# A fused transformer layer on one core: the softmax sums inverted three units later, the maxima split on VectorE, the next heads' operands loaded in parts

## The chip, the core and the metric

The kernel runs on one core of a Trainium2 chip. The core has five engines that each run their own instruction list in order and wait for one another by semaphores: TensorE (PE, matrix products; PEld is its weight load), VectorE (DVE), ScalarE (ACT), GpSimd (POOL) and SyncE (SP). SyncE computes nothing here: it issues all the DMA transfers, one after the other. TensorE writes to PSUM, which has eight banks of 128x512 float32; everything else lies in SBUF or in DRAM. The metric is the device time of one execution in microseconds (us).

## The reference

The layer adds three things to its input x (2048 rows, 512 columns): attention with 32 heads of width 16, a two-layer network with GELU (hidden width 1792), and x itself. Both branches read the same normalised x.

```
xn = layernorm(x)
qkv = (xn @ wqkv) in 32 heads of 16
p = softmax(q k^T * 16**-0.5) over 2048 keys;  o = p @ v
attention = o @ wo
mlp = gelu(xn @ w1 + b1) @ w2 + b2
out = x + attention + mlp
```

## The kernel before

**Precision.** Matrix operands are float16 pairs, a high part and the low part that it leaves, so that three products make one. Weights are scaled by powers of two from their largest value before they are split.

**Blocks and units.** Attention goes through eight groups of four heads, and within a group through four query blocks of 512 rows: 32 blocks, numbered t = 0 to 31. A block has 16 *units*. A unit (`unit`, L584) does two things. Its S half (`s_half`, L238) makes four 128x512 score tiles by TensorE and takes each one's row maxima by VectorE (L250): this is the first pass, which only finds the maxima. Its E half (`e_half`, L286) belongs to a block 20 units behind (`LEAD`): TensorE makes the scores again, transposed and with the maximum already subtracted, ScalarE takes the exponential (L297), and TensorE multiplies the result with v (`v_half`, L300), where a column of ones makes the sums of the exponentials as well. Between these halves TensorE gets a few products of the dense work (projections first, then the network's hidden and output layer, then the output projection).

**How the maxima get into the E half.** The operands of a group lie in SBUF "stacks" kst and qst (L79), 62 rows of q or k parts for the products, and two rows per head (62 and 63) that hold the maximum's two float16 parts in qst and a constant, 1024, in kst. At a block's last S unit `s_end` (L253) reduces the maxima to mneg (L261). One unit later `store` (L264) transposes mneg by TensorE into PSUM, VectorE scales it into msb (L271), GpSimd makes the high part and the low part, mhl (L274, L275), SyncE writes them to DRAM, m_d (L277, two transfers), and reads them back into rows 62 and 63 of qst (L282, four transfers). The block's E half needs these rows some four units later; its score products wait for qst<-m_d.

**How a block's sums are inverted.** When a block's last product with v is done, `v_end` (L313) copies the result to osb by ScalarE (L323) and sets up a chain with a due time for each step, counted in units: the sums to DRAM (L335) after 1, reshaped back into dn (L362) after 2, the inversion on VectorE (L338) after 2 + n, its result to DRAM (L340) one later, spread to rb (L344) after 3 + 2n, and then `store` (L346) after 4 + 3n: GpSimd multiplies osb by rb (L348), makes the float16 pair ot (L349, L350), and n units later `put` writes ot to DRAM, ot_d (L355, four transfers). n is 2, and 1 for the last four blocks.

**What sets the order.** TensorE, ScalarE, VectorE and GpSimd execute in the order in which the program issues their instructions. `later(n, f)` (L204) puts a step n units off, `tick` (L226) runs what is due, and `pooled` (L216) feeds GpSimd's steps by a budget of 2500 ns a unit. SyncE is not in this list (`ORDERED`, L40): the order of its transfers is made by the scheduler when the program is built, from its own idea of when operands and buffers become free; at run time the queue is strictly in order.

**Loading the stacks.** `stacks(g, w, blocks)` (L389) loads one operand of one group, four transfers of 48 KB a block. The stacks are held twice, for even and odd groups. Group 0 is loaded in the prologue; group 1, all 32 transfers, by the first call of `rest` (L855), which then writes the normalised x to DRAM, xn_d, in four transfers of 512 KB (L859); groups 2 to 7 by `more_stacks` (L1043), 32 transfers at once, when the E half has left the group that used the buffers.

**The prologue.** Units 0 to 15 (S only) run between the first projections. While they run, the weights pass by once in chunks (wch, L646) for their largest values (L650 on VectorE), and later once more to be split on GpSimd (L877 to L879). Units 16 to 19 have no E half yet; TensorE gets bursts of 8 to 16 products there.

Of the kernel before, what the change touches and what calls it, by code (L numbers as in the profile page):

```python
# [8 lines left out]
F32 = mybir.dt.float32  # L9
# [3 lines left out]
ALU = mybir.AluOpType  # L13
# [14 lines left out]
NQB = S // QB  # L28
NG = H // 4
VW = DH + 1  # L30
LEAD = 20
# [11 lines left out]
MROW = 1024.0  # L43
# [4 lines left out]
def layer_kernel(ctx: ExitStack, tc: tile.TileContext, x, wqkv, wo, w1, b1, w2, b2, out):  # L48
    nc = tc.nc
# [3 lines left out]
    def pool(stack, name, bufs=1, space=None, side=None):  # L53
        kw = {k: v for k, v in (("space", space), ("side", side)) if v is not None}
        return stack.enter_context(tc.tile_pool(name=name, bufs=bufs, **kw))

    const = pool(ctx, "const")
    work = pool(ctx, "work")
# [5 lines left out]
    xn_d = dram.tile([P, 2, NC, S], F16, name="xn_d")  # L64
# [42 lines left out]
    def banks(tag):  # L107
        k = free_banks[tag].pop(0)
        free_banks[tag].append(k)
        return bank_tile(k, tag)  # L110
# [48 lines left out]
    def given(engine, ns):  # L159
        backlog[engine] += ns  # L160
# [43 lines left out]
    def later(n, fn, local=False):  # L204
        queue.append((slot[0] + n, fn, local))
# [10 lines left out]
    def pooled(*todo):  # L216
        steps.extend(todo)
# [35 lines left out]
    def s_end(u):  # L253

        t, i = divmod(u, 16)
        if i < 15:
            return
        g, qb = divmod(t, NQB)
        qs = qst[g % 2]
        mneg = mnegs[t % 2]  # L260
        nc.vector.tensor_reduce(mneg[:, :16], mt_of[t].rearrange("p h t k -> p (h t) k"), axis=AX.X, op=ALU.max, negate=True)  # L261
        given("dve", 220)

        def store():  # L264

            pt = banks("S")
            for a in range(2):
                nc.tensor.matmul(pt[32 * a:32 * a + 32, :64], mneg[64 * a:64 * a + 64, :],
                                 ident[64 * a:64 * a + 64, 64 * a:64 * a + 64], start=True, stop=True)
            msb = work.tile([64, 64], F32, name="msb", bufs=2)  # L270
            nc.vector.tensor_scalar_mul(msb, pt[:64, :64], 1.0 / MROW)  # L271
            given("dve", 220)
            mhl = work.tile([64, 2, 64], F16, name="mhl", bufs=2)
            nc.gpsimd.tensor_scalar(mhl[:, 0], msb, 1.0, 0.0, op0=ALU.mult, op1=ALU.add)  # L274
            nc.gpsimd.tensor_tensor(mhl[:, 1], msb, mhl[:, 0], op=ALU.subtract)  # L275
            for a in range(2):
                nc.sync.dma_start(m_d[t, :, :, 64 * a:64 * a + 64], mhl[32 * a:32 * a + 16])  # L277
            for p in range(2):
                for a in range(2):
                    h = 2 * p + a  # L280
                    dst = qs[p][qb][64 * a + 62:64 * a + 64, :].rearrange("r (t q) -> r t q", q=P)
                    nc.sync.dma_start(dst, m_d[t, 4 * h:4 * h + 4].rearrange("t r q -> r t q"))  # L282

        later(1, store)
# [28 lines left out]
    def v_end(u):  # L313

        t, kt = divmod(u, 16)
        g, qb = divmod(t, NQB)
        for h in range(4):
            del ptiles[u, h]
        if kt < 15:
            return  # L320
        pv, k = pv_of.pop(t)
        osb = work.tile([P, QB], F32, name="osb", bufs=2)
        nc.scalar.activation(osb, pv, AF.Copy)  # L323
        given("act", 600)
        free_banks["S"].append(k)
        if t == NG * NQB - 1:
            later(1, lambda: last_one(osb))
            return

        dn = work.tile([64, 32], F32, name="dn", bufs=1)  # L330
        rb = work.tile([P, QB], F32, name="rb", bufs=1)

        def sums():
            for h in range(4):
                nc.sync.dma_start(den_d[t, 0, h:h + 1, :], osb[32 * h + DH:32 * h + DH + 1, :])  # L335

        def inverse():
            nc.vector.reciprocal(dn, dn)  # L338
            given("dve", 330)
            later(1, lambda: nc.sync.dma_start(den_d[t, 1].rearrange("h (c q) -> (h c) q", q=32), dn))  # L340

        def spread():
            for h in range(4):
                nc.sync.dma_start(rb[32 * h:32 * h + 32, :], den_d[t, 1, h:h + 1, :].to_broadcast([32, QB]))  # L344

        def store():  # L346
            ot = work.tile([P, 2, QB], F16, name="ot", bufs=2)
            pooled((1280, lambda: nc.gpsimd.tensor_tensor(osb, osb, rb, op=ALU.mult)),  # L348
                   (620, lambda: nc.gpsimd.tensor_scalar(ot[:, 0], osb, 1.0, 0.0, op0=ALU.mult, op1=ALU.add)),  # L349
                   (1160, lambda: nc.gpsimd.tensor_tensor(ot[:, 1], osb, ot[:, 0], op=ALU.subtract)),  # L350
                   (0, lambda: later(n, put)))

            def put():
                for h in range(4):
                    nc.sync.dma_start(ot_d[64 * g + DH * h:64 * g + DH * h + DH, :, qb * QB:(qb + 1) * QB],  # L355
                                      ot[32 * h:32 * h + DH])
                ready.add(t)


        n = 2 if t < (NG - 1) * NQB else 1  # L360
        later(1, sums)
        later(2, lambda: nc.sync.dma_start(dn, den_d[t, 0].rearrange("h (c q) -> (h c) q", q=32)))  # L362
        later(2 + n, inverse)
        later(3 + 2 * n, spread)
        later(4 + 3 * n, store)

    def last_one(osb):

        on = work.tile([P, 4, 4, DH], F32, name="on")
        rden = work.tile([P, 4, 4], F32, name="rden")  # L370
        pq = banks("S")
        for q in range(4):
            nc.tensor.transpose(pq[:, q * P:(q + 1) * P], osb[:, q * P:(q + 1) * P], ident)
        pqv = pq.rearrange("p (q h e) -> p q h e", q=4, h=4)
        nc.vector.reciprocal(rden, pqv[:, :, :, DH])
        nc.vector.tensor_tensor(on, pqv[:, :, :, 0:DH], rden.unsqueeze(3).to_broadcast([P, 4, 4, DH]), op=ALU.mult)
        pt = banks("S")
        for q in range(4):
            nc.tensor.transpose(pt[:64, q * P:(q + 1) * P], on[:, q].rearrange("p h d -> p (h d)"), ident)
        ot = work.tile([P, 2, QB], F16, name="ot", bufs=2)  # L380
        nc.scalar.activation(ot[:64, 0], pt[:64, :], AF.Copy)
        nc.vector.tensor_tensor(ot[:64, 1], pt[:64, :], ot[:64, 0], op=ALU.subtract)
        last.append(ot)
# [5 lines left out]
    def stacks(g, w, blocks):  # L389
        for b in blocks:  # L390
            for p in range(2):
                for a in range(2):
                    h = 4 * g + 2 * p + a
                    nc.sync.dma_start((qst, kst)[w][g % 2][p][b][64 * a:64 * a + 48, :],
                                      qk_d[w, h * DH:(h + 1) * DH, :, b * QB:(b + 1) * QB].rearrange("d j n -> (d j) n"))
# [69 lines left out]
    def by_slots(gen):  # L465

        def step():
            w = FINE
            while w == FINE:
                w = next(gen, 0)  # L470
            if w is None:
                later(1, step, True)

        later(1, step, True)
# [56 lines left out]
    pos, spent, cur = [0], [False], [None]  # L531
# [7 lines left out]
    def fetch_w1(n):  # L539
        if n < NQB * NF:  # L540
            wcs[n] = feed[0].tile([P, 2, NC, P], F16, name="wc", bufs=3)
            nc.sync.dma_start(wcs[n], w1_d[n % NF])
# [89 lines left out]
    with ExitStack() as st1:  # L632
# [3 lines left out]
        xt = ph.tile([P, 2, NC, S], F16, name="xt")  # L636
# [216 lines left out]
        feed.append(pool(ctx, "feed", side="right"))  # L853

        def rest():  # L855
            for w in (1, 0):
                stacks(1, w, range(NQB))
            for c in range(NC):
                nc.sync.dma_start(xn_d[:, :, c, :], xt[:, :, c, :])  # L859
            for m in range(1, 4):  # L860
                while m not in ready_w:
                    yield None
                if m < 3:
                    by_slots(prep_qk(m + 1, wfs[m + 1], sbank, ready_w))
                for sb in range(NQB):
                    for w in (1, 0):
                        yield project(m, w, sb, ready_w[m], dbank)
                    if m == 3 and sb == 2:
                        for n in range(2):
                            fetch_w1(n)  # L870
                        fetch_x(0)
# [166 lines left out]
                        lambda q=q: (yos[q], None), lambda yo, q=q: finish(yo, acs[q], qb * 4 + q), first=False)  # L1038

    yos = []  # L1040
    loaded = [1]

    def more_stacks():  # L1043

        e = pos[0] - LEAD
        while loaded[0] + 1 < NG and e > (loaded[0]) * 64:
            loaded[0] += 1
            for w in (1, 0):
                stacks(loaded[0], w, range(NQB))

    with ExitStack() as st2:
        st2p = pool(st2, "ph2")
# [5 lines left out]
    with ExitStack() as st3:  # L1058
# [35 lines left out]
        while pos[0] < NU + LEAD + 2:  # L1094
            more_stacks()
            unit(fil)
# [32 lines left out]
```

## Time and profile before

| | us |
|---|---|
| median of three runs | 1570.55 |
| lowest, highest run | 1565.78, 1573.75 |
| the profiled execution's own time | 1564.4 |
| its span, first to last instruction | 1562.6 |
| VectorE busy, of it row maxima (L250, 2048 instructions) | 1419.0, 1289.1 |
| ScalarE busy, of it exponentials (L297, 2048 instructions) | 1369.2, 1267.6 |
| GpSimd busy | 668.9 |

The mean granted clock of TensorE was 0.992 of full speed. Rows of the profile name an instruction by line, engine, operation and "out<-in" with the program's names; in lists of waits, "A <- B: 11.9, 3, 5.5" says that A waited for B 11.9 us in all, 3 times, 5.5 at most. In the timeline a row gives start, duration, engine, line, operation, shapes and count, and in brackets the idle time of the engine before it with what ended it. SyncE's rows are DMA issues; SPq is its sequencer. In rows by stretch, the columns are the stretch, its length, the busy time of PE, PEld, DVE, ACT and POOL (with counts), the granted clock, the share of the DMA engines and GB/s.

### The profile page before, as it was taken

What the parts mean: (1) busy time and instruction counts of PE and PEld (TensorE: products, weight loads), DVE (VectorE), ACT (ScalarE), POOL (GpSimd) and SP (SyncE); (2) the same over time, 40 slices, a digit from 0 to 9 for tenths busy, and PEclk for the clock granted to TensorE, in tenths of its full rate; (3) what the DMA queues carried; (4) which work ended last, traced back from release to release, by engine and by line L of the source; (5) the groups of instructions that cost most, each with busy time, mean ns of one, the idle gap of its engine ahead of it and who ended that gap; (6) DMA issues with size and microseconds to landing.
All of it is one profiled execution on the core that took longest, in us unless ns stands there. A gap on an engine that the chain in (4) does not pass through costs nothing.

```text
span 1562.6 us, 85974 instructions
## 1 busy us (share of the span) xinstructions
PE 1509.6 (97%) x38915; PEld 813.5 (52%) x38915; DVE 1419.0 (91%) x2388; ACT 1369.2 (88%) x2254; POOL 668.9 (43%) x742
## 2 busy tenths in 40 slices
PE   8997998989999999999999999999999999999998
PEld 4433554545555555555555555555555555554543
DVE  8886987989999999999999999999999999999911
ACT  4314997989999999999999999999999999999993
POOL 3113587737773111777411167751127773111000
PEclk9998999999999999999999999999999999999999
DMA  6467466351121111121111111221112100003123
GB/s 205 129 205 257 130 172 211 114 167 47 47 67 50 38 34 36 58 57 44 55 44 50 34 45 43 64 63 37 40 41 66 42 21 28 29 21 125 55 91 103
DMA packets 120248, 123.71 MB, mean 79 GB/s; under 512 B 38988, under 2 KB 90572, under 8 KB 119880
## 3 DMA queue, kind: packets, MB, share of 16 engines
q1 hardware_dynamic: 119880, 118.21, 25.0%
q8 instruction: 304, 4.98, 1.3%
q14 instruction: 64, 0.52, 0.1%
HBM read 80.61 MB, written 37.34 MB: 75 GB/s over the span
## 4 chain that ended last, share of the span: by engine, by line
PE 70%; DVE 21%; DMA 4%; issue 2%; POOL 1%; SPq 1%; ACT 1%; DVEq 0%; POOLq 0%
PE pV L169 21%; DVE mt L250 16%; PE pD L169 16%; PE pS L169 15%; PE pT L169 14%; DVE hh L978 2%; PE pD L428 1%; DMA wch<-in_B_w_dram 1%; PE pT L428 1%; DVE amx L650 1%; DMA dn<-den_d 1%; PE pT L521 1%; DMA m_d<-mhl 0%; PE pS L428 0%; DMA out_dram<-ac 0%
## 5 line engine op out<-in xcount | busy, mean ns | idle before, releaser
L297 ACT ACTIVATE pe<-pT,sexp 128x512 f32<-128x512 f32 x2048 | 1267.6, 688 | 72.8 <-PE pT L169 26.9
L250 DVE TENSOR_REDUCE mt<-pS 128x1 f32<-128x512 f32 x2048 | 1289.1, 683 | 34.4 <-PE pS L169 15.6
L169 PE MATMUL pV<-pe,vv 64*32 64x512 f32 x8192 | 1079.0, 597 | 1.4 <-PE pS L169 0.7
L169 PE MATMUL pT<-qst,kst 64*32 64x512 f16 x8192 | 706.9, 379 | 3.9 <-DMA qst<-m_d 1.4
L169 PE MATMUL pS<-kst,qst 62*32 62x512 f16 x8192 | 636.1, 379 | 35.6 <-DVE mt L250 32.1
L169 PEld LDWEIGHTS <-qst 62*32 62x32 f16 x8192 | 280.2, 92 | 273.5 <-issue 136.2
L169 PEld LDWEIGHTS <-kst 64*32 64x32 f16 x8192 | 294.1, 91 | 176.5 <-issue 68.6
L169 PE MATMUL pD<-w_s,g 64*32 64x512 f16 x5376 | 364.8, 377 | 0.0
L169 PE MATMUL pD<-xb,wc 64*32 64x512 f16 x5376 | 361.4, 378 | 0.0
L169 PEld LDWEIGHTS pV<-pe,vv 64*32 64x32 f32 x8192 | 181.6, 105 | 96.7 <-PE pS L169 7.6
L169 PEld LDWEIGHTS <-wc 64*32 64x32 f16 x5376 | 120.5, 92 | 52.6 <-issue 2.7
L169 PEld LDWEIGHTS <-g 64*32 64x32 f16 x5376 | 111.4, 91 | 44.4 <-issue 0.2
L169 PE MATMUL pD<-xt,wqk_h 64*32 64x512 f16 x1920 | 127.4, 382 | 0.7 <-issue 0.7
L996 POOL TENSOR_TENSOR xa<-xa,yt 128x512 f32<-128x512 f32 x16 | 20.4, 1276 | 238.8 <-ACT yt L994 238.8
L958 POOL TENSOR_TENSOR t<-hh 128x512 f32<-128x512 f32 x56 | 58.2, 1038 | 112.0 <-DVE hh L978 110.7
L348 POOL TENSOR_TENSOR osb<-osb,rb 128x512 f32<-128x512 f32 x31 | 39.9, 1286 | 150.5 <-DMA rb<-den_d 150.5
L274 POOL TENSOR_SCALAR mhl<-msb 64x64 f16<-64x64 f32 x32 | 7.6, 237 | 175.4 <-DVE msb L271 175.4
L960 POOL TENSOR_TENSOR t<-t,hh 128x512 f32<-128x512 f32 x56 | 71.7, 1280 | 4.7
L953 POOL TENSOR_TENSOR t<-t,hh 128x512 f32<-128x512 f32 x56 | 71.6, 1279 | 4.7
L955 POOL TENSOR_TENSOR g<-t,g 128x512 f16<-128x512 f32 x56 | 65.1, 1163 | 4.6
L169 PEld LDWEIGHTS <-wqk_h 64*32 64x32 f16 x1920 | 43.8, 93 | 16.1 <-issue 1.3
L169 PE MATMUL pD<-wo_s,oc 64*32 64x512 f16 x768 | 50.1, 378 | 0.0
(138 smaller groups left out, 869.5 us busy)
## 6 DMA issues: line engine op xcount, KB each, us to landing
wch<-in_B_w_dram SPq DMA_DIRECT2D x28, 512.0 KB
wc<-w_d SPq DMA_DIRECT2D x56, 256.0 KB
qk_d<-stg SPq DMA_DIRECT2D x32, 256.0 KB
rb<-den_d SPq DMA_DIRECT2D x124, 64.0 KB
kst<-qk_d SPq DMA_DIRECT2D x128, 48.0 KB
qst<-qk_d SPq DMA_DIRECT2D x128, 48.0 KB
xs<-in_A_x_dram SPq DMA_DIRECT2D x16, 256.0 KB
qk_d<-stg SPq DMA_DIRECT2D x32, 128.0 KB
```

Source lines behind the costliest of these rows:

```text
L169: p = nc.tensor.matmul(*args, **kw)
L250: nc.vector.reduce_max(mt_of[t][:, n, qt, kb:kb + 1], s, axis=AX.X)
L297: nc.scalar.activation(pe, st, AF.Exp, scale=sexp[:, g // 2:g // 2 + 1])
L348: pooled((1280, lambda: nc.gpsimd.tensor_tensor(osb, osb, rb, op=ALU.mult)), (620, lambda: nc.gpsimd.tensor_scalar(ot[:, 0], osb, 1.0, 0.0 ...
L428: nc.tensor.matmul(self.bank, lhs, rhs, start=start, stop=self.last and self.over())
L521: nc.tensor.matmul(pj, xt[:, i, c, t * P:(t + 1) * P], wh[j][:, c, :], start=(n == 0), stop=(n == 11))
L953: (1280, lambda: nc.gpsimd.tensor_tensor(t1, t1, hh, op=ALU.mult)),
L955: (1160, lambda: nc.gpsimd.tensor_tensor(g[:, 1, f, :], t1, g[:, 0, f, :], op=ALU.subtract)),
L958: pooled((1040, lambda: nc.gpsimd.tensor_tensor(t1, hh, hh, op=ALU.mult)), (620, lambda: nc.gpsimd.tensor_scalar(t1, t1, 1.0, 1.0 / GELU_A ...
L960: (1280, lambda: nc.gpsimd.tensor_tensor(t1, t1, hh, op=ALU.mult)),
L978: nc.vector.tensor_scalar(hh, hp, scale, bias, op0=ALU.mult, op1=ALU.add)
L996: add = lambda: nc.gpsimd.tensor_tensor(xa, xa, yt, op=ALU.add)
```

## The change

Three edits:

1. In `v_end` the inversion, its spreading and the product with it come three units later, in all but the last four blocks. The steps keep their distances from the inversion on; the sums' way to dn is not moved.
2. In `store` of the maxima, VectorE makes both float16 parts straight from PSUM: the high part by the scaling that made msb, the low part by a second instruction that scales the same PSUM values again and subtracts the high part. msb and GpSimd's two steps are gone. The book-keeping of VectorE's load (`given`) goes from 220 to 300 ns.
3. The stacks of a next group are loaded in eight parts, four transfers a unit, k's four blocks first. For group 1 that is from the first unit after the prologue on, with the four xn_d writes behind it, one a unit; for the later groups from three units after the E half has entered a group.

```diff
@@ s_end, store
-            msb = work.tile([64, 64], F32, name="msb", bufs=2)
-            nc.vector.tensor_scalar_mul(msb, pt[:64, :64], 1.0 / MROW)
-            given("dve", 220)
             mhl = work.tile([64, 2, 64], F16, name="mhl", bufs=2)
-            nc.gpsimd.tensor_scalar(mhl[:, 0], msb, 1.0, 0.0, op0=ALU.mult, op1=ALU.add)
-            nc.gpsimd.tensor_tensor(mhl[:, 1], msb, mhl[:, 0], op=ALU.subtract)
+            nc.vector.tensor_scalar_mul(mhl[:, 0], pt[:64, :64], 1.0 / MROW)
+            nc.vector.scalar_tensor_tensor(mhl[:, 1], pt[:64, :64], 1.0 / MROW, mhl[:, 0], op0=ALU.mult, op1=ALU.subtract)
+            given("dve", 300)
@@ v_end
-        n = 2 if t < (NG - 1) * NQB else 1
+        n, far = (2, 3) if t < (NG - 1) * NQB else (1, 0)
         later(1, sums)
         later(2, lambda: nc.sync.dma_start(dn, den_d[t, 0].rearrange("h (c q) -> (h c) q", q=32)))
-        later(2 + n, inverse)
-        later(3 + 2 * n, spread)
-        later(4 + 3 * n, store)
+        later(2 + n + far, inverse)
+        later(3 + 2 * n + far, spread)
+        later(4 + 3 * n + far, store)
@@ rest
-            for w in (1, 0):
-                stacks(1, w, range(NQB))
+            for k in range(8):
+                later(1 + k, lambda k=k: stacks(1, 1 - k // 4, [k % 4]), True)
             for c in range(NC):
-                nc.sync.dma_start(xn_d[:, :, c, :], xt[:, :, c, :])
+                later(9 + c, lambda c=c: nc.sync.dma_start(xn_d[:, :, c, :], xt[:, :, c, :]), True)
@@ more_stacks
-    loaded = [1]
+    loaded = [0]
...
-        e = pos[0] - LEAD
-        while loaded[0] + 1 < NG and e > (loaded[0]) * 64:
+        g, k = divmod(loaded[0], 8)
+        if g + 2 < NG and pos[0] - LEAD >= 64 * (g + 1) + 3:
             loaded[0] += 1
-            for w in (1, 0):
-                stacks(loaded[0], w, range(NQB))
+            stacks(g + 2, 1 - k // 4, [k % 4])
```

In the changed program as built, the lines after these edits stand up to three lines higher.

## The prediction

> **What bounds the kernel now.** I read the page first, then the waits by engine, then the timeline around the longest waits of VectorE, and last the queue of SyncE. "Unit" is the step of the schedule in which four 128x512 score tiles are reduced (S) and four tiles of a block 20 units behind are exponentiated (E); a "block" is sixteen units (front section).
>
> ```profile
> PE 1509.6 (97%) x38915; PEld 813.5 (52%) x38915; DVE 1419.0 (91%) x2388; ACT 1369.2 (88%) x2254; POOL 668.9 (43%) x742
> 390.00:440.00 50.00, 49.08 (x1399) 27.04 (x1400) 49.56 (x84) 47.97 (x81) 38.21 (x42) 1.00 0.16 43
> 520.00:570.00 50.00, 49.91 (x1402) 28.49 (x1396) 49.25 (x82) 48.26 (x80) 6.08 (x7) 1.00 0.11 32
> ```
>
> The two stretches (us; then PE, PEld, DVE, ACT, POOL busy) show a kernel without slack: in the hidden-layer stage (390 to 440) VectorE works 49.56 of 50 us, in the output-layer stage (520 to 570) TensorE 49.91. Every engine runs a fixed order, so a wait of TensorE or VectorE in a unit is lost for good, nearly in full. What can be won are the few idle times:
>
> ```profile
> DVE dn L338 <- DMA dn<-den_d: 11.9, 3, 5.5
> DVE amx L650 <- DMA wch<-in_B_w_dram: 9.3, 2, 8.3
> ```
>
> (engine and line, what it waited for, us in all, times, longest.) Two of the three waits for dn and one for a weight chunk are long; the rest of the span is dense. SyncE's queue has waits of its own, and these will matter:
>
> ```profile
> SPq L355 <- POOL ot L350: 154.7, 27, 14.3
> ```
>
> SyncE stands 154.7 us at L355, in 27 blocks, until GpSimd has finished ot. It issues in order: whatever is behind waits as well. Today that harms little.
>
> **The change, part by part.** The sum is made against the profiled execution, 1564.4 us (span 1562.6); the median of the three runs, 1570.55, lies 6.15 above it.
>
> *Loads of the next heads in parts.* SyncE's order is chosen by the scheduler as operands become free, and in the built programs the stack loads of the later head groups hardly change places. What does change is the start: the four xn_d writes, today ahead of a weight chunk and of the first m_d, go behind the first qst<-m_d; the chunk goes ahead of all sixteen qst loads.
>
> ```profile
> 106.20 7.39 SPq L394 DMA_DIRECT2D qst<-qk_d  x16
> 113.64 4.14 SPq L859 DMA_DIRECT2D xn_d<-xt  x4
> 117.87 1.33 SPq L646 DMA_DIRECT2D wch<-in_B_w_dram  x1
> ...
> 129.22 0.69 DVE L650 TENSOR_REDUCE amx<-wch 128x1 f32<-128x512 f32 x1 [8.29 <-DMA wch<-in_B_w_dram]
> ...
> 118.93 2.77 PE L428 MATMUL pT<-xt,wqk_h 128*128 128x512 f16 x12
> ...
> 131.11 4.56 PE L428 MATMUL pD<-xt,wqk_h 128*128 128x512 f16 x12
> ```
>
> The chunk is issued at 117.87 and lands at 129.22; VectorE idles 8.29 us. Issued near 106, it has over 14 us before VectorE wants it at 120.9, against the 11.35 us that it took even behind all the other transfers: the wait goes. After it twelve products took 4.56 us, the same twelve before it 2.77: 1.79 more. Gain 8.29 + 1.79 = **10.1**. What is late next is the first E unit's qst<-m_d, wanted 10.1 us sooner than today; the xn_d writes no longer stand in front of it. Bounds: 6 (I allow it to be late by 4) to 11.4 (the whole landing time is won).
>
> *Inversion three units later.* Sums, inversion, spread and product of a block all keep their distances; inversion, spread, product and the ot_d writes move by three units.
>
> ```profile
> 249.77 0.53 SPq L362 DMA_DIRECT2D dn<-den_d  x1
> ...
> 255.13 0.34 DVE L338 RECIPROCAL dn<-dn 64x32 f32<-64x32 f32 x1 [5.52 <-DMA dn<-den_d]
> ...
> 258.89 1.29 DVE L250 TENSOR_REDUCE mt<-pS 128x1 f32<-128x512 f32 x2 [1.08 <-PE pS L169]
> 261.35 2.02 DVE L250 TENSOR_REDUCE mt<-pS 128x1 f32<-128x512 f32 x3 [1.17 <-PE pS L169]
> ...
> 348.87 0.35 DVE L338 RECIPROCAL dn<-dn 64x32 f32<-64x32 f32 x1 [4.94 <-DMA dn<-den_d]
> ...
> 352.63 0.69 DVE L250 TENSOR_REDUCE mt<-pS 128x1 f32<-128x512 f32 x1 [1.08 <-PE pS L169]
> ```
>
> Three units are 8 us (the m_d rows of blocks 18 and 19 below lie 44.69 us apart, sixteen units of 2.79), more than 5.52 or 4.94: both waits go, and with them the slow matmuls behind them. Gain 5.52 + 1.08 + 1.17 + 4.94 + 1.08 = **13.8**; not below 11 (half of the after-effects stays). The third wait, about 1.4, is in one of the last four blocks, which keep their distances.
>
> *Maxima's parts on VectorE.* Per block one VectorE instruction more, reading PSUM and the part before it, and two fewer on GpSimd.
>
> ```profile
> L271 DVE TENSOR_SCALAR msb<-pS 64x64 f32<-64x64 f32 x32 | 6.8, 212 | 5.5 <-PE pS L268 2.5 <-PE pT L169 1.7 <-PE pS L169 0.7
> L338 DVE RECIPROCAL dn<-dn 64x32 f32<-64x32 f32 x31 | 10.4, 335 | 11.9 <-DMA dn<-den_d 11.9
> ```
>
> No row has this form. The nearest, L271, is 212 ns; it is at hand in 32 blocks, and VectorE is the limit in about ten (the hidden-layer stage): 10 x 0.21 = **2.1** lost. Ends: 32 x 0.335 = 10.7 with L338's price everywhere; below nothing by 3, if the shorter way to m_d (GpSimd ends mhl 0.70 us behind msb) helps blocks whose E waits today.
>
> *What the later inversion pushes.* This is where I differ from reading the change as a gain. In the changed order the four ot_d writes of block t-2 stand ahead of the m_d writes of block t in most blocks, as today, but their data now comes 8 us later, and m_d is what the E stage of block t needs. Block 19 today:
>
> ```profile
> 966.32 1.17 POOL L350 TENSOR_TENSOR ot<-osb,ot 128x512 f16<-128x512 f32 x1
> 970.59 0.24 POOL L274 TENSOR_SCALAR mhl<-msb 64x64 f16<-64x64 f32 x1 [3.10 <-DVE msb L271]
> ...
> 967.51 2.48 SPq L355 DMA_DIRECT2D ot_d<-ot  x4
> ...
> 971.23 1.50 SPq L277 DMA_DIRECT2D m_d<-mhl  x2
> 974.33 1.18 SPq L282 DMA_DIRECT2D qst<-m_d  x4
> ...
> 978.95 1.26 ACT L297 ACTIVATE pe<-pT,sexp 128x512 f32<-128x512 f32 x2
> ```
>
> ot is ready at 967.5, its writes are out at 970.0, and m_d leaves at 971.23 as soon as mhl is there. Put the product at 972.2 and ot at 975.4 (three units on; in the changed GpSimd order one more run of GELU steps stands ahead of the product): the writes take 2.48, m_d leaves at 977.9, 6.7 late. The room: qst<-m_d ends its issue at 975.51, E begins at 978.95, 3.44 later. How much of that the landing needs is shown by block 18, where today two ot_d writes stand between m_d and qst<-m_d:
>
> ```profile
> 926.54 1.23 SPq L277 DMA_DIRECT2D m_d<-mhl  x2
> 930.86 1.18 SPq L355 DMA_DIRECT2D ot_d<-ot  x2
> 932.14 1.30 SPq L282 DMA_DIRECT2D qst<-m_d  x4
> ...
> 933.88 0.10 PEld L169 LDWEIGHTS <-kst 64*32 64x32 f16 x4 [1.52 <-DMA qst<-m_d]
> ...
> 934.54 0.69 DVE L250 TENSOR_REDUCE mt<-pS 128x1 f32<-128x512 f32 x1 [0.73 <-PE pS L169]
> 935.62 1.29 DVE L250 TENSOR_REDUCE mt<-pS 128x1 f32<-128x512 f32 x2 [0.39 <-PE pT L169]
> ```
>
> There the product begins 0.44 after the issue's end, its exponential some 0.5 later: the landing needs 1.0, the room in block 19 is 2.4, and TensorE waits 6.7 - 2.4 = 4.3. Block 18 also shows the price: TensorE's loader waits 1.52, VectorE loses 0.73 + 0.39 = 1.12, so 0.4 of each wait is absorbed. I carried this subtraction through all blocks, with each block's own rows and the changed orders of GpSimd and SyncE. First and last of thirteen:
>
> ```profile
> 370.33 1.19 SPq L277 DMA_DIRECT2D m_d<-mhl  x2
> 374.78 1.18 SPq L282 DMA_DIRECT2D qst<-m_d  x4
> ...
> 378.06 1.27 ACT L297 ACTIVATE pe<-pT,sexp 128x512 f32<-128x512 f32 x2
> ...
> 1276.03 1.18 SPq L277 DMA_DIRECT2D m_d<-mhl  x2
> 1279.90 1.15 SPq L282 DMA_DIRECT2D qst<-m_d  x4
> ...
> 1283.05 1.94 ACT L297 ACTIVATE pe<-pT,sexp 128x512 f32<-128x512 f32 x3
> ```
>
> Block 5: ot at 374.5, m_d 6.7 late, room 1.1, wait 5.6. Block 26: ot at 1277.0, 3.5 late, room 1.0, wait 2.5. All: blocks 5, 7, 8, 11, 12, 14, 16, 18, 19, 21, 24, 25, 26 wait 5.6, 4.7, 3.5, 1.5, 5.0, 1.3, 0.3, 0.4, 4.3, 1.8, 5.0, 2.4, 2.5 = 38.3 (in 11, 18 and 25 it is qst<-m_d that stands behind an ot_d write). In the others ot comes in time, or the writes stand behind qst<-m_d. Less 13 x 0.4 = 5.2.
>
> Waits also cool the clock. After the idle times of 5.2 and 4.7 us that the dn waits gave TensorE, the granted clock (third column from the end) was low:
>
> ```profile
> 256.00:261.00 5.00, 4.92 (x80) 2.33 (x83) 3.10 (x6) 2.44 (x4) 1.52 (x2) 0.50 0.60 168
> 349.50:354.00 4.50, 4.18 (x80) 1.96 (x79) 3.34 (x6) 1.94 (x3) 0.00 (x0) 0.62 0.25 71
> ```
>
> It cost 2.25 and 1.08 there. Five of the thirteen waits are 4.3 or more; I count a quarter of them at 1.7: 2. The Trainium skill ("TensorE: Matmul & The Clock Gate", Part 1) has the clock halved after an idle window of about 3.4 us that runs free of the program. By that rule alone all five could be hit, and the term would be 8.5 in place of 2; the two rows agree with the rule, but no row here shows what an idle time of about 4 us does.
>
> Term: 38.3 - 5.2 + 2 = **35.1** lost, from 12 (only blocks whose m_d is 6 or more late) to 50 (the bare shift of three units, without GpSimd's new order, in every block).
>
> Sum: 1564.4 - 10.1 - 13.8 + 2.1 + 35.1 = 1577.7, 13.3 more than before; on the median 1570.55 + 13.3 = **1584**.
>
> **The rivals.**
>
> *The writes are out in time.* GpSimd loses its wait for msb (3.10 in the row above), and the product could start as soon as rb has landed. It decides from the point where the product starts as many us sooner as TensorE would wait: in block 19 4.3 sooner than 972.2, and m_d is late by no more than the room. For it speaks that the product waits for rb alone where no GELU steps stand ahead; against it, that in the changed GpSimd order they do. Then only 10.1 + 13.8 - 2.1 = 21.8 of gain is left: 1549, faster.
>
> *Half absorbed.* If the landing needs less than 1.0, or GpSimd catches up after the first waits, the term is 15 in place of 35.1, the sum 13.3 - 20.1 = -6.8: 1564 on the median, no change.
>
> *The start isn't won.* If the chunk is held by the transfers and not by its place, or the first qst<-m_d is late, 10.1 is missing: 1594.
>
> *The inversion still waits.* If dn comes over 8 us late, the change doesn't do what it says: 13.8 is missing, 1598. Against it: 5.52 is the longest of 31.
>
> **How the numbers follow.** Forecast 0.55; writes in time 0.13; half absorbed 0.15; start not won 0.12; inversion waits 0.05. The forecast's own range is 1566 to 1602, by the bounds of its terms. With the others, 1556 to 1602 leaves out the fast rival and a little above. About 0.5% is what a measurement of this kernel can tell from no change, 1562.7 to 1578.4. Faster: 0.13, half of the second rival, and a little, 0.21; same: the other half and 0.3 of the forecast, 0.25; slower: 0.54.
>
> **What would show it.** VectorE's waits at L338 for dn fall from 11.9 to about 1.5, and at L650 from 9.3 to 1 (gain steps right). TensorE or its loader waits for qst<-m_d over 25 us in ten or more blocks, and SyncE waits longer for ot ahead of m_d (loss step right). If instead m_d leaves within 1 us of mhl in most blocks, the loss step is wrong, and the time is near 1549. If VectorE still idles over 3 us before a weight chunk (L650) at the start, the first term is wrong.

## The result and the profile after

The changed kernel takes **1654.45 us** (median of six runs, 1650.72 to 1660.64); the kernel before took 1568.15 beside it (six runs). The ratio is 1.0557 (95% interval 1.0525 to 1.0590). The profiled execution took 1654.47 us, 90.07 more than that of before; the mean granted clock fell from 0.992 to 0.976. The direction of the forecast was right, its size (13.3 us) was not.

The page of the changed kernel, span and busy time:

```profile
span 1652.7 us, 85954 instructions
PE 1545.0 (93%) x38915; PEld 820.7 (50%) x38915; DVE 1427.7 (86%) x2420; ACT 1371.7 (83%) x2254; POOL 652.4 (39%) x678
```

VectorE and ScalarE are busy for nearly as long as before (8.7 and 2.5 us more); their shares fell from 91% and 88% to 86% and 83% because the span grew. So most of the 90 us is time in which they wait. The waits of the changed kernel (engine and line, what it waited for, us in all, times, longest):

```profile
DVE mt L250 <- PE pS L169: 112.4, 82, 6.4
...
PEld L169 <- DMA qst<-m_d: 79.6, 24, 6.5
...
PE pT L169 <- DMA qst<-m_d: 64.3, 21, 6.1
...
DVE dn L336 <- DMA dn<-den_d: 1.7, 1, 1.7
...
DVE amx L648 <- DMA wch<-in_B_w_dram: 0.5, 1, 0.5
...
SPq L353 <- POOL ot L348: 176.8, 29, 10.9
```

The two waits that the change was forecast to remove are gone: for dn 1.7 us are left of 11.9, for the weight chunk 0.5 of 9.3. In their place TensorE's loader waits 79.6 us for qst<-m_d, in 24 blocks; in the profile of before these rows read

```profile
PEld L169 <- DMA qst<-m_d: 4.0, 5, 1.5
PE pT L169 <- DMA qst<-m_d: 1.4, 3, 0.8
```

Two of these blocks in the changed kernel's timeline (start, duration, engine, line, transfer or operation, count; in brackets the idle time before it). First the queue of SyncE at block 16, then block 19, the one that the prediction worked out:

```profile
887.99 2.48 SPq L353 DMA_DIRECT2D ot_d<-ot  x4
890.57 2.80 SPq L392 DMA_DIRECT2D kst<-qk_d  x4
893.46 1.19 SPq L275 DMA_DIRECT2D m_d<-mhl  x2
895.87 1.16 SPq L280 DMA_DIRECT2D qst<-m_d  x4
...
1026.72 1.29 POOL L346 TENSOR_TENSOR osb<-osb,rb 128x512 f32<-128x512 f32 x1
...
1028.81 1.17 POOL L348 TENSOR_TENSOR ot<-osb,ot 128x512 f16<-128x512 f32 x1
...
1030.00 2.58 SPq L353 DMA_DIRECT2D ot_d<-ot  x4
...
1032.68 1.18 SPq L275 DMA_DIRECT2D m_d<-mhl  x2
...
1035.08 1.15 SPq L280 DMA_DIRECT2D qst<-m_d  x4
...
1036.70 0.10 PEld L169 LDWEIGHTS <-kst 64*32 64x32 f16 x4 [4.46 <-DMA qst<-m_d]
...
1037.37 0.69 DVE L250 TENSOR_REDUCE mt<-pS 128x1 f32<-128x512 f32 x1 [3.57 <-PE pS L169]
...
1038.62 1.29 DVE L250 TENSOR_REDUCE mt<-pS 128x1 f32<-128x512 f32 x2 [0.56 <-PE pS L169]
```

In block 19 mhl was ready at 1024.94. SyncE stands at ot_d until ot ends (1029.98), issues four writes, and only then m_d, at 1032.68: 7.7 us late. The loader waits 4.46, where the prediction had 4.3. Block 16 is the other kind: behind the late ot_d writes stand four loads of the next group's k as well, and m_d leaves 5.8 us after mhl (887.64). Before, SyncE issued ot_d and these loads in its idle time while mhl was not ready yet:

```profile
831.29 2.48 SPq L355 DMA_DIRECT2D ot_d<-ot  x4
833.87 3.92 SPq L394 DMA_DIRECT2D kst<-qk_d  x6
840.42 1.19 SPq L277 DMA_DIRECT2D m_d<-mhl  x2
842.83 1.16 SPq L282 DMA_DIRECT2D qst<-m_d  x4
```

The clock around block 19 in the changed kernel, by stretches (us; PE, PEld, DVE, ACT, POOL busy; granted clock; DMA share; GB/s):

```profile
1030.00:1035.00 5.00, 2.83 (x72) 1.09 (x59) 3.80 (x6) 2.86 (x6) 3.86 (x5) 1.00 0.13 28
1035.00:1040.00 5.00, 3.30 (x72) 1.98 (x80) 1.98 (x3) 2.48 (x4) 2.78 (x3) 0.79 0.35 96
1040.00:1045.00 5.00, 5.00 (x136) 3.12 (x121) 3.54 (x6) 3.65 (x8) 0.10 (x1) 0.87 0.02 6
```

From 1040 on TensorE works without a pause, but at 0.87, and VectorE still gets only 3.54 us of work in five: the price of the wait runs on behind it.

Lining up the starts of the same units in both traces tells where the 90 us arise (us; a plus is time lost; an "E unit" is one with an E half, and a block's first E unit is the one that needs the new rows of qst):

```
unit 18 to 20, chunk and stack loads at the start       -8.1
units 26 to 28                                          +5.7
units 57 to 59 and 89 to 90, the two waits for dn      -12.8
first E unit of 20 blocks                              +95.1
units 237 and 346                                       +5.9
the rest, spread                                        +4.3
sum                                                    +90.1
```

### The profile page after: what moved, and what is told of

It is laid out like the page before. It is cut to its first block, busy times and chain, and to the rows that moved or that the text cites. A ratio compares the mean times of both kernels' runs of the same rounds, so it can differ in the third digit from the quotient of the medians.

```text
span 1652.7 us, 85954 instructions
## 1 busy us (share of the span) xinstructions
PE 1545.0 (93%) x38915; PEld 820.7 (50%) x38915; DVE 1427.7 (86%) x2420; ACT 1371.7 (83%) x2254; POOL 652.4 (39%) x678
## 3 DMA queue, kind: packets, MB, share of 16 engines
q8 instruction: 304, 4.98, 1.3%
## 4 chain that ended last, share of the span: by engine, by line
PE 66%; DVE 20%; DMA 5%; issue 3%; POOL 3%; SPq 2%; ACT 1%; DVEq 0%; POOLq 0%
PE pV L169 20%; DVE mt L250 15%; PE pD L169 15%; PE pS L169 14%; PE pT L169 13%; DMA m_d<-mhl 3%; DVE hh L976 2%; DMA qst<-m_d 2%; PE pD L426 1%; PE pT L426 1%; DVE amx L648 1%; PE pT L519 1%; SPq L353 0%; POOL osb L346 0%; POOL ot L348 0%
## 5 line engine op out<-in xcount | busy, mean ns | idle before, releaser
L169 PE MATMUL pV<-pe,vv 64*32 64x512 f32 x8192 | 1098.4, 606 | 1.1 <-PE pS L169 0.7
L169 PE MATMUL pS<-kst,qst 62*32 62x512 f16 x8192 | 657.6, 385 | 20.6 <-DVE mt L250 14.6
L169 PEld LDWEIGHTS <-kst 64*32 64x32 f16 x8192 | 291.8, 91 | 252.5 <-DMA qst<-m_d 79.6
L169 PE MATMUL pD<-w_s,g 64*32 64x512 f16 x5376 | 370.9, 381 | 2.1 <-issue 2.1
L169 PE MATMUL pD<-xb,wc 64*32 64x512 f16 x5376 | 369.5, 384 | 0.6 <-issue 0.6
L169 PEld LDWEIGHTS pV<-pe,vv 64*32 64x32 f32 x8192 | 187.9, 106 | 102.5 <-PE pS L169 7.6
L169 PE MATMUL pD<-xt,wqk_h 64*32 64x512 f16 x1920 | 131.6, 387 | 4.0 <-issue 4.0
L950 POOL TENSOR_SCALAR t<-t,gs 128x512 f32<-128x512 f32 x56 | 38.8, 693 | 24.0 <-ACT t L945 24.0
```

Of the source, the lines that this page charges most:

```text
L169: p = nc.tensor.matmul(*args, **kw)
L950: pooled((690, lambda: nc.gpsimd.tensor_scalar(t1, t1, 1.0, gs[:, 1:2], op0=ALU.add, op1=ALU.mult)), (1280, lambda: nc.gpsimd.tensor_tenso ...
```

## The experiments

**The theory** after the result: m_d waits in SyncE's queue behind ot_d writes whose ot comes late. That needs two things at once, the order and the lateness. **Rivals**: the later inversion does it whatever the order is; the order does it without a late ot; VectorE's new instruction or the transfers of edit 3 do it. "Ahead" below is the number of ot_d writes of block t-2 that SyncE's list, as built, has in front of m_d of block t. Each ratio is to the kernel before, run beside it on the same chip.

**Each edit by itself, and edits 2 and 3 together.** The first kernel is before with only

```diff
-        later(2 + n, inverse)
+        later(2 + n + far, inverse)
```

and its two companions, far = 3 (0 in the last four blocks).

> The kernel before with edit 1 alone (inversion, spread and product three units later). Theory: the loss needs both a late ot and ot_d writes that stand ahead of m_d in SyncE's order. As built here, no ot_d write stands ahead of m_d in blocks 2 to 29; in 15 of these blocks one or two stand between m_d and qst<-m_d. So the dn waits go (13.8 us gained), and the 15 blocks lose 0 to 2 us each: within 1% of before, 1550 to 1585 us, VectorE's wait for dn below 3 us, TensorE's loader waits for qst<-m_d 5 to 35 us instead of 79.6. Rival (the later inversion alone does it, whatever the order): 1640 or more, loader waits over 60 us.

The second is before with VectorE making both parts of the maxima, as in the changed kernel:

```diff
-            nc.gpsimd.tensor_scalar(mhl[:, 0], msb, 1.0, 0.0, op0=ALU.mult, op1=ALU.add)
-            nc.gpsimd.tensor_tensor(mhl[:, 1], msb, mhl[:, 0], op=ALU.subtract)
+            nc.vector.tensor_scalar_mul(mhl[:, 0], pt[:64, :64], 1.0 / MROW)
+            nc.vector.scalar_tensor_tensor(mhl[:, 1], pt[:64, :64], 1.0 / MROW, mhl[:, 0], op0=ALU.mult, op1=ALU.subtract)
```

> The kernel before with edit 2 alone (VectorE makes both parts of the maxima). As built, all four ot_d writes of the block two before stand ahead of m_d in every block. Theory: ot is there early enough, since the inversion is where it was, so m_d is late by little: 1560 to 1585 us (2 us for the instructions, a few us where ot ends after mhl). Rival (the instructions on VectorE or their port are what costs): 1600 or more, with VectorE waits unchanged and its busy time up by over 20 us. Second rival (the order alone does it, without a late ot): 1610 or more with loader waits for qst<-m_d over 40 us.

The third is before with the diff of `rest` and `more_stacks` only.

> The kernel before with edit 3 alone (stacks in parts, xn_d writes behind). SyncE's order of ot_d and m_d is that of before in all blocks. Theory: the start is won, less what the later xn_d transfers cost around the sixth E unit (5.7 us in the changed kernel): 1558 to 1568 us, 0.1 to 0.6% faster. Rival (the parts or their traffic make the loss): over 1600.

The fourth is the changed kernel with `far` taken out again.

```diff
-        n, far = (2, 3) if t < (NG - 1) * NQB else (1, 0)
+        n = 2 if t < (NG - 1) * NQB else 1
```

> The changed kernel with the inversion put back to its old place (edits 2 and 3 without 1). As built, all four ot_d writes stand ahead of m_d in every block, as in the run with edit 2 alone. Theory: ot is early, so no more than a few us of waits: 1555 to 1580 us, loader waits for qst<-m_d below 25 us, dn waits back at about 12 us. Rival (edit 2 or 3 or the two together do it): 1620 or more, loader waits over 50 us.

Measured (median, ratio with interval, loader's wait for qst<-m_d in the profiled run):

```
edit 1 alone      1566.13   0.9987 (0.9972 to 1.0002)   10.7
edit 2 alone      1596.32   1.0184 (1.0156 to 1.0213)   36.8
edit 3 alone      1563.19   0.9975 (0.9961 to 0.9990)    3.8
edits 2 and 3     1588.66   1.0130 (1.0093 to 1.0167)   34.8
all three         1654.45   1.0557 (1.0525 to 1.0590)   79.6
```

Edit 1 alone loses nothing, so the first rival falls. Edit 2 alone loses 29 us, 11 more than the theory's upper end and 14 less than the second rival's lower one: the order costs something even without the later inversion. Edits 2 and 3 together missed in the same way, 9 us above the theory's upper end, with 34.8 us of waiting where it had under 25. Where the waits lie still fits the theory: 25.3 of the 36.8 us with edit 2 alone are in blocks 2, 3, 6, 13, 18, 20 and 25, the seven in which the kernel before had no ot_d write ahead of m_d. In these ot is late without edit 1 (it ends between 0.8 us before mhl and 1.8 us behind it; in the others it ends 1.3 to 10 us before mhl), and edit 2 puts its writes ahead. Another 8.8 us are in blocks 1 and 4, which ot does not explain: block 1 has no ot_d, and in block 4 ot ends 5.3 us before mhl. From edits 2 and 3 (1.30%) and edit 1 (-0.13%) one would add up 1.17%; all three give 5.57%. The missing 4.4%, 69 us, exist only where edits 1 and 2 meet. The waits of the kernel with edit 1 alone:

```profile
PEld L169 <- DMA qst<-m_d: 10.7, 12, 1.5
...
DVE dn L338 <- DMA dn<-den_d: 2.3, 1, 2.3
```

Block 18 of the kernel with edit 2 alone shows the turned order. In before, the prediction quoted the same block with m_d ahead of ot_d, at 926.54:

```profile
941.87 0.22 DVE L272 SCALAR_TENSOR_TENSOR mhl<-pS,mhl 64x64 f16<-64x64 f32 x1
...
942.69 1.16 POOL L348 TENSOR_TENSOR ot<-osb,ot 128x512 f16<-128x512 f32 x1
...
943.88 2.50 SPq L353 DMA_DIRECT2D ot_d<-ot  x4
...
946.48 0.53 SPq L540 DMA_DIRECT2D wc<-w_d  x1
...
947.11 1.19 SPq L275 DMA_DIRECT2D m_d<-mhl  x2
...
953.18 0.11 PEld L169 LDWEIGHTS <-kst 64*32 64x32 f16 x4 [4.54 <-DMA qst<-m_d]
```

mhl is there at 942.09, ot at 943.85, and m_d leaves at 947.11. The orders as built make the pattern plain. Before: in 7 of the blocks 2 to 29 no ot_d write is ahead of m_d, in the others all four are. Edit 1 alone: none ahead in any of them. Edit 2 alone: all four ahead in every block. All three edits: none ahead in 8 blocks, three in one, all four in the others. So edit 1 pushes the ot_d writes back in SyncE's list and edit 2 pushes m_d back; together they leave the order much as it was, while at run time ot comes 8 us later and mhl does not.

**Taking the wait out of SyncE's queue.** Two ways: ot_d issued by GpSimd, or m_d and qst<-m_d issued by GpSimd.

```diff
-                    nc.sync.dma_start(ot_d[64 * g + DH * h:64 * g + DH * h + DH, :, qb * QB:(qb + 1) * QB],
+                    nc.gpsimd.dma_start(ot_d[64 * g + DH * h:64 * g + DH * h + DH, :, qb * QB:(qb + 1) * QB],
```

> The changed kernel, all three edits, with the four ot_d writes of a block issued by GpSimd in place of SyncE, so that nothing on SyncE waits for ot. Theory (m_d stands behind ot_d writes whose ot comes late): TensorE's loader waits for qst<-m_d fall from 79.6 us to under 25 (block 1 has no ot_d ahead of it and keeps its 4.7), time 1550 to 1580 us. Rival (m_d is held by something else in SyncE's queue, such as the write of the inverse, for which SyncE waits 148 us in all): the waits stay over 50 us and the time over 1620.

```diff
-                nc.sync.dma_start(m_d[t, :, :, 64 * a:64 * a + 64], mhl[32 * a:32 * a + 16])
+                nc.gpsimd.dma_start(m_d[t, :, :, 64 * a:64 * a + 64], mhl[32 * a:32 * a + 16])
...
-                    nc.sync.dma_start(dst, m_d[t, 4 * h:4 * h + 4].rearrange("t r q -> r t q"))
+                    nc.gpsimd.dma_start(dst, m_d[t, 4 * h:4 * h + 4].rearrange("t r q -> r t q"))
```

> The changed kernel, all three edits, with m_d<-mhl and qst<-m_d issued by GpSimd in place of SyncE; ot_d stays on SyncE, and ot stays as late as it is. Theory (the place in SyncE's queue is all that costs): loader waits for qst<-m_d under 12 us, VectorE's waits for dn under 3 us, VectorE's extra instruction 6.9 us of work: 1545 to 1562 us, faster than before by 0.3 to 1.4%. Rival (the late sums, the transfers or VectorE's new instruction cost by themselves, without the queue): over 1590. If GpSimd's own order delays m_d (it is busy with GELU in the hidden-layer stage), the waits come back in blocks 4 to 28: 1565 to 1600.

And the changed kernel with edit 2 taken back (msb and GpSimd's two steps return):

> The changed kernel with the maxima's parts back on GpSimd (edits 1 and 3 without 2). As built, no ot_d write stands ahead of m_d in blocks 2 to 29, as with edit 1 alone. Theory (edit 2 turns the order round, edit 1 makes the turned order dear): the sum of the runs with edits 1 and 3 alone, 1556 to 1566 us, loader waits under 20. Rival (edits 1 and 3 meet at the start or in the sums' chain): over 1575.

With ot_d off SyncE: 1569.15 us, ratio 1.0011 (0.9997 to 1.0025); the loader's wait is

```profile
PEld L169 <- DMA qst<-m_d: 14.5, 6, 4.6
```

so 65 of the 79.6 us of waiting and 85 us of time hang on that one place in the queue. That brings the time back to that of before, not to what edits 1 and 3 reach without edit 2 (1558.70, below): of the 96 us between that and the changed kernel 85 go with ot_d's place, and by the units' starts the rest arises in the first hundred units, of it 6.9 us at block 1. All three edits are still there, VectorE's instruction and edit 3's transfers too: the rivals that blame these by themselves fall. The 4.6 is block 1, as expected.

With m_d off SyncE: 1574.94 us, ratio 1.0050 (1.0030 to 1.0070), 13 us above the range that the theory gave, and within that of the third case. Its waits:

```profile
POOL m_d L275 <- DVE mhl L272: 288.5, 32, 28.7
...
POOL qst L280 <- DMA m_d<-mhl: 71.7, 30, 3.9
...
PEld L169 <- DMA qst<-m_d: 20.1, 16, 2.2
```

m_d now leaves within 0.3 us of mhl in every block, and no wait is longer than 2.2. But GpSimd stands 71.7 us until m_d has landed, and qst<-m_d follows m_d late where GpSimd is busy; one queue is exchanged for another. Why its median is so much above its own profiled run (1568.43) stays open.

Without edit 2: 1558.70 us, ratio 0.9946 (0.9928 to 0.9964), waits 11.2 us, dn 4.2. Edits 1 and 3 together are a gain, as the theory had it.

**The version that follows.** Two waits for dn were long, those of blocks 1 and 3. So: edits 1 and 3, and the later inversion in these two blocks alone.

```diff
-        n, far = (2, 3) if t < (NG - 1) * NQB else (1, 0)
+        n = 2 if t < (NG - 1) * NQB else 1
+        far = 3 if t in (1, 3) else 0
```

> Edits 1 and 3 without 2, and the inversion later in blocks 1 and 3 alone, the two whose long waits for dn edit 1 is to remove. As built, SyncE's order of ot_d and m_d is that of before in all blocks but two. Theory: the two dn waits are all that edit 1 wins (11 us), and the 6 to 8 us that the run with edits 1 and 3 gives back after unit 92 come from ot_d writes between m_d and qst<-m_d, which are now as before: 1.5 + 11 + the start's 2.4 less a little, 1552 to 1558 us, 0.6 to 1.0% faster than before. Rival (what comes back after unit 92 has another cause): no better than the run with edits 1 and 3, 1559 to 1563.

Measured: **1548.28 us**, ratio 0.9894 (0.9876 to 0.9912), 1.06% faster than before and better than the 1552 to 1558 expected. Its waits:

```profile
PEld L169 <- DMA qst<-m_d: 2.1, 3, 1.5
...
DVE dn L338 <- DMA dn<-den_d: 1.5, 1, 1.5
```

What edits 1 and 3 gave back late in the span is kept, since the ot_d writes between m_d and qst<-m_d are again where they were. It beats both kernels.

**What edit 3 gives back at the start.** The kernel just measured, with xn_d moved:

```diff
-                later(9 + c, lambda c=c: nc.sync.dma_start(xn_d[:, :, c, :], xt[:, :, c, :]), True)
+                later(20 + 3 * c, lambda c=c: nc.gpsimd.dma_start(xn_d[:, :, c, :], xt[:, :, c, :]), True)
```

> The kernel of the run before this one, with the four xn_d writes issued by GpSimd, three units apart, from the twentieth unit after the prologue on; xb is first used at 310 us. Theory: the 3.9 to 5.7 us that edit 3 gives back in units 26 to 28 come from the 2 MB of xn_d and of xb that fill the DMA engines there, so they are not lost: 3 to 5 us less than the run before this one. Rival (the units are late for another reason, the chunks' or q and k transfers): no difference, and the same TensorE idle time of about 2 us near 153 us.

Measured: 1556.09 us, ratio 0.9936 (0.9922 to 0.9951): not 3 to 5 us less, but 8 more. The two stretches in question, in the version with the two blocks (xn_d on SyncE):

```profile
150.00:155.00 5.00, 4.04 (x114) 2.24 (x121) 2.85 (x6) 2.73 (x6) 0.94 (x1) 1.00 0.94 265
155.00:160.00 5.00, 1.86 (x65) 0.80 (x53) 1.71 (x4) 1.45 (x3) 0.00 (x0) 1.00 0.36 124
```

and with xn_d moved away:

```profile
150.00:155.00 5.00, 5.00 (x154) 2.85 (x154) 4.65 (x10) 4.34 (x8) 0.00 (x0) 1.00 0.17 57
155.00:160.00 5.00, 5.00 (x152) 3.00 (x137) 5.00 (x12) 5.00 (x9) 3.03 (x4) 1.00 0.17 58
```

The idle time is gone, and by the units' starts about 5 us are won there. So the transfers of xn_d and of xb, which is read back from it, cost this time; moving xn_d moved both, and which of them it is was not separated. The forecast of the sum was wrong, because SyncE's list changed elsewhere: xb<-xn_d, 1 MB, which stood at 148 us, is now issued at 217.26, and the six transfers and the chunk between it and block 2's m_d take up to 2.1 us each to issue.

```profile
217.26 1.42 SPq L538 DMA_DIRECT2D xb<-xn_d  x1
...
219.95 5.09 SPq L915 DMA_DIRECT2D w_d<-wsp  x4
225.10 1.48 SPq L647 DMA_DIRECT2D wch<-in_B_w_dram  x1
226.68 1.24 SPq L277 DMA_DIRECT2D m_d<-mhl  x2
```

m_d leaves 8.3 us after mhl (218.42), and TensorE's loader waits 5.7. The units around block 2's first E unit lose 10 us, and block 18's another 3. It is the same fault as in the changed kernel, a late m_d in SyncE's queue, from another edit.

**How much lateness costs, and what the instruction costs.** The changed kernel with one unit in place of three, `(2, 1)` for `(2, 3)`:

> The changed kernel with the inversion one unit later in place of three. As built, all four ot_d writes stand ahead of m_d in every block, as in the run without edit 1 (1588.7 us) and unlike the changed kernel, where seven blocks have none. Theory (the loss is the time at which ot comes, through the queue): more blocks wait than without edit 1, each up to 2.8 us more: 1600 to 1645, loader waits 45 to 80 us. Rival (a later ot costs nothing by itself, the changed kernel's order in single blocks does it): within 1% of the run without edit 1, below 1600.

1612.51 us, ratio 1.0294 (1.0275 to 1.0314), waits 59.8 us in 18 blocks: between no unit (1588.66, 34.8) and three (1654.45, 79.6), as the theory had it. And the best kernel with the added VectorE instruction and nothing else of edit 2:

```diff
+            low = work.tile([64, 64], F16, name="low", bufs=2)
+            nc.vector.scalar_tensor_tensor(low, pt[:64, :64], 1.0 / MROW, msb, op0=ALU.mult, op1=ALU.subtract)
-            given("dve", 220)
+            given("dve", 300)
```

> The kernel of the run with the inversion later in two blocks (1548.3 us, 1.06% faster than before), with edit 2's second VectorE instruction added but nothing taken from GpSimd: it reads the same PSUM values and msb and writes a tile that nobody reads. SyncE's order of ot_d and m_d stays. Theory (the instruction is hidden but in the ten blocks or so where VectorE is the limit): 2 us more, 1550.4, ratio to before 0.989 to 0.992. Rival (VectorE's time counts in all 32 blocks): 7 to 11 us more, 1555 to 1559, ratio 0.994 or above. Second rival (the wider booking of VectorE's load in the planner moves other work): a change of more than 3 us either way with VectorE's waits changed.

1552.63 us, ratio 0.9919 (0.9904 to 0.9933) against 0.9894 (0.9876 to 0.9912): 0.25%, 4 us, though the intervals overlap. The ratio lies in the theory's range and below the rival's 0.994. The instruction itself:

```profile
L273 DVE SCALAR_TENSOR_TENSOR low<-pS,msb 64x64 f16<-64x64 f32 x32 | 6.9, 216 | 1.1
```

The 4 us are not shown to be this instruction's. In the profiled runs, 4.2 us apart over the S units, the units in which it runs and the ones behind them add up to 0.8 us (in most blocks its 0.25 us are made up for in the next unit); 3.7 us arise in units 10, 47 and 489, in which it does not run. VectorE's waits for pS are unchanged (19.2 us against 19.0), so there is no sign of the second rival either.

## Why the prediction was right or wrong, point by point

**The start** (-10.1, bounds 6 to 11.4). The wait went, and units 18 to 20 are 8.1 us shorter. What was not in the sum is that the xn_d writes, issued at 126 to 140 us in place of 113 to 118, and the load of xb behind them (147 in place of 137) now run beside the first E units: 5.7 us come back in units 26 to 28. Net 2.4, below the lower bound; edit 3 alone gains 0.25%. "What is late next" was looked for in the first qst<-m_d, not in the xn_d writes that were moved. These are 4 MB: the list of DMA issues has 1024 KB for each of the four, twice what the front section says, and twice the 2 MB in the expectation of the run that moves them.

**The dn waits** (-13.8, not below 11). 12.8 in the changed kernel, 13.3 in the same units with edit 1 alone, where 2.3 come back in the units right behind. Right. (With half of the after-effects left the lower end would be 12.1, not 11.)

**VectorE's instruction** (+2.1, -3 to 10.7). No more than about 4, and by the units' starts nearer to 1. Within its bounds; 216 ns where the nearest row was 212. As two instructions edit 2 was priced rightly; what it cost came through SyncE's list (next point).

**What the later inversion pushes** (+35.1, 12 to 50). This is the step that failed: the mechanism, the place and the worked block were right, the size was not. It measured 95.1, 60 more: 13.7 in the listed blocks, 27.6 in blocks that the prediction took for harmless ("in the others ot comes in time, or the writes stand behind qst<-m_d"), and 18.7 in the after-effects. In detail:

- The thirteen listed blocks: 38.3 us forecast, 52.0 measured (loader's waits). Where only ot_d stood ahead of m_d the subtraction holds: blocks 5, 12, 19 and 24 wait 5.8, 5.8, 4.5 and 5.3 against 5.6, 5.0, 4.3 and 5.0. It fails where more is queued behind ot_d: block 16 waits 3.2 against 0.3, since four loads of the next group come between. The issue time of each of these adds to m_d's lateness; the forecast moved the ot_d writes and not what had been filling SyncE's idle time behind them.
- ot itself: about 8 us later in the median of 28 blocks, as forecast (8), but up to 13, where rb or the write of the inverse waits in the same queue. Block 22, not listed, waits 4.1: its ot is some 12 later.
- Eleven blocks not counted: 27.6 us, of which blocks 1, 2 and 4 make 15.5 (4.7, 6.5, 4.2). In block 2 no ot_d write stood ahead of m_d before, and all four do now; block 1 has no ot_d at all, there m_d stands behind four w_d writes and a chunk. These waits are there with edit 2 alone (4.8, 8.0, 4.0). The prediction put this term under edit 1 and looked at edit 2 as two instructions; it gave no price to the place that edit 2 gives m_d in SyncE's list.
- The after-effects: -5.2 absorbed and +2 for the clock were forecast, together -3.2. A wait after which the clock holds is absorbed as forecast (block 10: the loader waits 2.95, its unit is 2.7 longer). But 13 of the 24 waits were followed by half clock, not a quarter of five, and their units grew by 1.6 us more than the whole wait on average: together some 16 us lost where 3 were to be saved. The price for each, 1.7, was about right; the number was not. The Trainium skill ("TensorE: Matmul & The Clock Gate", Part 1) halves the clock after an idle window of about 3.4 us. The forecast weighed this rule and put it aside in favour of a quarter; here the rule was the better guide, and even it is too mild, as the last section shows.

**The rivals.** "The writes are out in time" would have had m_d within the room in most blocks; it left over 1 us late in 19 of the blocks 1 to 27. "Half absorbed" fell with the waits. The other two would have added 10 and 14; none had a mechanism worth 80. The forecast's own range, 1566 to 1602, is said to follow from the bounds of its terms; added up they give 1554 to 1614, and 1654 lies outside that as well.

**The cause, settled and open.** That m_d's place behind ot_d costs the time is shown from three sides: ot_d off the queue (1569.15), edit 2 taken back (1558.70), the inversion taken back (1588.66). Why the scheduler puts m_d later when VectorE makes its parts was not tried; at run time mhl is complete 0.25 us after the end of VectorE's first instruction, against 0.71 before, so the list and the chip go opposite ways.

## What to carry to other kernels

In a queue that issues in order, the cost of a later operand is not its own lateness: it is that of every transfer listed behind it, and what counts is the slack of the most urgent of these. When an edit moves a producer to another engine, read the built order of the DMA queue, not only of the engines, and try the edits one at a time: here two edits that by themselves changed the time by -0.1% and +1.8% made 5.6% together, beside a third that gains. An edit that removes a rare wait belongs only in the blocks that have it: beside edit 3, the later inversion in 2 of 28 blocks gave 1.06%, in all of them 0.54%.

## What the runs showed of the hardware

**Less than a whole step of idle time halves the clock.** In the traces' clock records the halved stretches begin on a grid of 3.41 us and last whole steps of it. TensorE's idle time was added up within each full-clock step between 100 and 1490 us, over the thirteen traces (some 5200 steps): each of the 39 steps with more than 1.95 us of it was followed by half clock, from 1.40 to 1.95 it was 20 of 45, below 1.40 none. So in the changed kernel a wait of 2.5 us that falls into one step is enough (block 16), and one of 2.8 that is split into 0.9 and 1.9 does nothing (block 21). The mean clock of 0.976 against 0.992 comes from these stretches: 80.9 us at half clock against 27.0.

**TensorE can run out of instructions.** TensorE's idle time under "issue", in which it waits for nothing that the profile shows, is 2.60 us ahead of unit 27 in the changed kernel:

```profile
156.95 0.39 PE L169 MATMUL pD<-xt,wqk_h 64*32 64x512 f16 x2 [2.60 <-issue]
```

The page of that kernel lists a DMA queue of its own kind:

```profile
q8 instruction: 304, 4.98, 1.3%
```

4.98 MB in 304 packets of 16 KB. TensorE has 2 x 38,915 = 77,830 products and weight loads, which makes 64.0 bytes each; at 256 to a packet 304 packets hold 77,824. The name and the sizes say that this queue brings TensorE's instructions; the waits below fit that. Its packets come some 4.6 us apart. Where the other transfers fill the engines the next one is late: in the changed kernel packets begin at 147.03 and 154.66, 7.6 us apart, with the DMA engines 92% busy from 145 to 155; with xn_d moved away they begin at 145.59, 149.01, 153.16 and 157.28, and the idle time is gone. In the thirteen traces there are 50 "issue" waits of TensorE of over 0.6 us; each ends 1.2 to 1.6 us after such a packet has landed. The two losses at units 237 and 346 of the changed kernel (2.1 and 2.06 us idle) are of this kind too. There the packets came 9.2 and 8.4 us apart with the DMA engines about half busy. In both, SyncE had issued a load of xb, 1 MB, 8.8 and 8.6 us before TensorE went on; and of the 50 waits all 14 that lie after 300 us come 6.9 to 9.9 us after such a load. Not every load of xb is followed by one, and why a load that leaves the engines half free holds a packet back is open.
